# All eight feature pairs of one group's first layer as seven half-size products, with a new written order of the whole kernel

## The chip, the cores and the metric

The kernel runs on one core of one Trainium2 chip. The metric is the device time of one execution in microseconds (us). Timed runs of the kernel before give a median of 292.01 us (291.48 to 292.09, three runs). The profile comes from one more execution, which took 292.66 us; the span of its instructions, from the first to the last, is 290.9 us.

## What is computed

Attention with two kinds of window (q, k, v: 8 batches, 8 heads, 576 positions, 64 features a head), then two matrix layers with a Silu between them. Cut to what matters:

```python
scores = scale * np.matmul(q, k.transpose(0, 1, 3, 2))
# heads 0-3: rel in [0, 32); heads 4-7: rel in [0, 128) and rel % 4 == 0
scores = np.where(masks[None], scores, -1e9)
attn = softmax(scores); attn_out = attn @ v
x = attn_out.transpose(0, 2, 1, 3).reshape(4608, 512)
h = x @ w_in                      # 512 x 2048
g = h * (1.0 / (1.0 + np.exp(-h)))
return g @ w_out                  # 2048 x 512
```

All operands of the matrix engine are float16 on the chip, sums are float32.

## The kernel before, in words

**Stages.** The 8 batches of attention feed a table of features xA (128 partitions, 4 parts of the 512 features, a ring of 2048 tokens). The 4608 tokens are worked off in ten groups: groups 0 and 1 of 256 tokens, groups 2 to 9 of 512. For each group, layer 1 makes gT (16 blocks of 128 hidden features by the group's tokens) and layer 2 makes the output rows. Attention of later batches runs between the matrix layers of earlier groups. Batches 0 to 2 bring their operands into shape by transposes on PE, batches 3 to 7 by a cast into DRAM (POOL's queue) and transposing DMAs (SP's queue). Batches 5 to 7 also send their result to DRAM and take it back transposed (steps W and X, SP's queue).

**Two ways of layer 1.** A standard block (`l1`, line 834; matmuls on line 839) is four matmuls of the group's width (512 columns for group 7), one for each part of the 512 features, and then one Silu on ACT (line 848) or, in mode t, a Tanh on ACT and a DVE instruction (lines 851 and 853). A fast pair (`l1_fast`, line 894; matmuls on line 927) makes two blocks at once by the seven products of Strassen's scheme: the blocks' weights, the features and the tokens are each cut in half, and seven products of two matmuls of 256 columns take the place of eight such half products (eight matmuls of 512 columns). The scheme needs sums of weight halves S1 to S4 (steps a0, a2, a4, a6, each for two pairs, line 879) and of feature halves T1 to T4 (steps t7, t8, t9, line 890). Products 0, 2, 4 and 6 of a pair go to its first bank of PSUM, products 1, 3 and 5 to its second. Products 0 to 2 are copied out (line 935, by ACT or DVE as the order says), and after products 3, 4 and 5 a DVE addition (line 943) joins one of the copies to what the bank holds by then. ACT applies Silu to three pieces: 256 columns after product 6 (line 939), 256 after product 4 (946) and 512 after product 5 (949). So a product must wait until the reader of the product two before it has left the bank. Which pairs are fast is set by `FAST1`: pairs 4 to 7 of group 7 and all eight of groups 8 and 9.

**Layer 2.** From group 2 on it uses the same scheme (`layer2_fast`, line 1013; line 1024), with sums of gT as steps u (line 990, mostly DVE). Results are added on DVE (line 1050) into output buffers ob, three in rotation, and stored from SP's or ACT's queue (line 1059; line 1052 for halves of the last tile).

**The order.** Nothing is scheduled by a program: `TABLE` is a list of steps, and each engine and each queue gets its instructions in that order. A step's name is given several times: the first time issues its matmuls, the next times its followers on the other engines, one each. What stands after "=" is, the first time, the PSUM bank (a, b, x, y, u, z; s is a double bank; a fast pair names two banks and a digit for its set of temporaries), and later the engine or queue (A: ACT, D: DVE, P: POOL, S: SP). `l7.4.0=by1` is product 0 of pair 4 of group 7; `l7.2=a` and `l7.2=s` are a standard block and its Silu; `7S1` are scores of batch 7, with exp on ACT and a mask multiplication on DVE; `7P0` and `7D0` are products with v; `7XP0`, `7XD0`, `7W0`, `7X0` bring features out; `7T` is one transposing DMA and `7L` loads for batch 7; `y7.0.3` is product 3 of tile 0 of group 7's layer 2; `f6` is a one-element copy on POOL that reads gT (a fence); `z` with a number is a filler: one idle matmul of 512 columns (line 1091) that keeps PE's clock up while it waits.

Of the kernel before, what the change touches and what calls it, by code (L numbers as in the profile page):

```python
# [11 lines left out]
0N0=D z15 z2 0N1=A z1 z25 0N3=D z21 z0 0TD2=b 0N2=A 0TD1=z 0TD1=A 0TD2=D 0TD3=x 0TD3=A 0TD0=u 0TA1k=a 0TD0=D  # L12
0TA1k=A 0S3=s 0S3 0TA1q=x 0TA0q=z 0TA0q=D z9 0TA1q=A 0TA0k=a 0TA0k=A 0S3 0S4=s 0S4 0S0=bz 0S4 0D0=u 0S1=s 0S0
0S0 0D1=z 0TR=x 0D0 0D1 0O0 0D0 0S1 0TR=A 0S1 0P1=b 0TR=A 0S6=au 0S6 0S5=s 0N10=D 0S6 0S5 0S5 0N6=D 0P0=a
0TS0=x 0D1 0TS0=A 0P1 0P1 0TS1=b 0O2 0D2=u 0P0 0D4=z 0TS1=A 0TS1=A 0P0 0TS0=A 0XP1=b 0XP1=A 0S2=s 0D2 0D2 0S2
0D4 0XP2=a 0D4 0O1 0XP0=u 0S2 0XP0=A 0D3=b z28 0XD0=y 0XD0=A 0D3 0D3 0P3=x 0P3 0P2=u 0P2 0XP2=A 0XD0=A l0.0=b
0P2 0P3 0XD1=u 0XD1=D 0XD1=D l0.0=s 0M 0XP3=a l0.3=z l0.7=x 0XP4=b 0XP4=D 0XP5=u 0XP5=D l0.7=t 0B 0XP3=D
l0.3=s l0.1=y l0.7 l0.6=b l0.1=s l1.6=z l1.6=t l1.4=a l1.4=t 0N7=D l0.2=u l1.6 l0.6=t l0.6 l1.11=y l1.11=s
l1.4 l1.7=z l0.2=s l1.3=x l1.7=s l1.0=y l0.8=b l0.11=u l1.0=s 0N4=A l0.8=s l0.11=t l0.11 l0.9=y l1.10=z l0.9=s
l1.3=s l1.10=s l1.8=b l1.1=u l0.5=x l1.15=a l1.1=s l1.15=s l1.2=y l0.5=s l1.9=u l1.9=s 0N8=D l1.12=x l0.13=a  # L20
l1.12=s 1TD3=z l1.8=s l1.2=s l0.12=x l0.12=t l0.4=b l0.4=s 1TD3=D l0.13=t l0.12 0B 1TD1=u 1TD1=D 1TS1=y 1TS1=A
0N5=A 1TA1q=z l0.13 1TS1=A l1.5=b 1TD2=u 1TA1q=A l1.5=s 1TD0=x l0.14=y 1TD2=D l0.14=s l0.10=a l0.10=s 1TD0=D
1TA1k=x 1TA0q=b 1S3=s 1S3 1TA1k=D 1TA0q=D 1TA0k=u 1TA0k=D 1TS0=x y0.1.0=z 1TS0=D 1TS0=D 1S1=au 1S1 1V1=D 1O2
1S2=bx 1S2 1S3 y0.0.0=y 1S3 1S2 1S2 1S4=s l0.15=a 1S1 1S4 l1.14=b l1.13=u 1V0=D 1S4 1S4 1S0=s l0.15=t y0.0.1
y0.1.1 l0.15 1D1=a 1S1 l1.14=s 1D1 1D1 1D2=x y1.0.0=b y1.0.1 1D4=a 1D4 l1.13=s 1D0=u y0.1.2 1S0 1S0 1S0 1D4
1D2 y0.1.3 1D0 1D0 1D2 y0.0.2 y0.0.3 1O0 y0.0.3=A 1P3=u 1P3 w1 1P0=x 1P0 0N9=D y1.0.2 1P0 y1.1.0=y 0B 1P3
1P1=x y0.1.3=A 1XP0=a 1P1 1P1 1XP0=D 1P2=z 1P2 y1.0.3 1P2 y0.0.3=A 1D3=u y1.1.1 y1.0.3=A 1D3 1XP2=z 3T 1XP1=a
3T 1D3 1XP2=D 1XD0=b 1XP1=A 1XD0=D 1XD0=A 1XD1=u y1.1.2 1XD1=D 1XD1=D 1XP3=x 1XP3=A 1XP5=z 1XP5=D 2TD0=b
2TD1=a 2TD2=z 2TD3=u 2TD2=D 2TD1=A 2TD3=A y1.1.3 2TD0=D 1XP4=a 2S4=s 1XP4=D y1.1.3=A 2TA0k=b 2TA0k=D 2S4
2TA1k=a 3T 2TA0q=z 2TA1q=y 2S4 2TA1q=D 2TA0q=A 2TS1=x 2TS0=u 2TS0=A 2TS1=D l2.10=b 2S3=s 2TS1=A 2TS0=A 2V1=D  # L30
2S2=zy l2.10=t 2S3 2S3 2S2 2TA1k=D l2.0=x 2S2 l2.10 2S1=ba 2S3 2S1 2S1 2S0=s 2S0 2S4 l2.8=u 2S2 l2.8=s l2.2=y
l2.2=s 2V0=D 2D1=z l2.1=b 2D1 2D1 l2.14=a l2.1=s l2.6=z l2.6=s l2.3=u 2S0 2S1 l2.3=s 2D0=b l2.14=t 2S0 w0
2D2=y l2.4=z l2.4=s 3T w1 w1 2D0 2D0 l2.0=s w0 l2.15=u l2.15=s l2.5=z l2.5=s 2D2 2D2 l2.14 2P1=b y1.0.3=A 2P1
2P0=y 2P1 l2.11=u l2.11=s 2XD0=x 2P2=b w0 l2.7=z l2.7=s 2P0 2P0 l2.12=y 2P2 2P2 y0.1.3=A 2XP1=b 2D4=u 2XD0=A
2XD0=A l2.9=a u2.2=D l2.12=s 2D4 y1.1.3=A 2D4 l2.9=s 2XP1=D l2.13=z l2.13=s 3L 2D3=x 2XP2=b 2XP2=A 2XP0=u
u2.0=D y2.0.0=y 2D3 2D3 y2.0.0=D 2XP0=A 2XP3=x 2XP3=D 2XD1=a 2P3=z 2P3 2XD1=A u2.2=D 3S1=s u2.0=D 2XD1=A v0
# [36 lines left out]
6P3 y6.0.2=A u6.1=D y6.0.3 y6.0.4 7S2 7S2 y6.0.4 7S4=s 7S4 7D0=b y6.0.3 a4=D 7P0=y 7D0 y6.0.6 6P3 y6.0.6=A 7D0
# [44 lines left out]
def kernel(  # L118
# [1013 lines left out]
```

## Time and profile before

| | |
|---|---|
| median of three runs | 292.01 us (291.48 to 292.09) |
| the profiled execution | 292.66 us |
| its span | 290.9 us |
| TensorE clock granted, mean | 0.998 |
| matmuls | 3034, the last one starts at 287.2 us |
| line 839 (standard blocks) | 480 matmuls, 352 of 512 columns |
| line 927 (fast pairs) | 280 matmuls of 256 columns |
| DVE, ACT busy | 217.9, 189.3 us |

PE is the matrix engine and PEld its weight loads, DVE the vector engine, ACT the one for functions, POOL the general one, SP the one that only issues DMAs. In the timeline and in the chain, the columns are the start, the duration and what ran. The chain follows the work that ended last back to what released each step. A matmul's own duration includes its way through the array (379 ns for 512 columns, 273 for 256), so its rate is read from starts.

### The profile page before, as it was taken

How to read it: one execution, taken by the hardware profiler on the slowest of the kernel's cores; microseconds unless marked ns; L12 is line 12 of the kernel's file. 1: busy time of each engine (PE TensorE's matmuls, PEld its weight loads, DVE VectorE, ACT ScalarE, POOL GpSimd, SP SyncE). 2: the span in 40 equal slices, each digit the busy share in tenths (PEclk: the TensorE clock that was granted, in tenths of full speed). 3: DMA queues.
4: the chain of work that ended last, by engine and by line, in shares of the span. 5: the costliest groups of instructions: out<-in, count | busy, mean ns of one | idle time of the engine just before them, and what ended most of it. 6: DMA issues, size and time to landing. Idle time of an engine off the chain costs nothing.

```text
span 290.9 us, 7524 instructions
## 1 busy us (share of the span) xinstructions
PE 284.4 (98%) x3034; PEld 205.5 (71%) x3034; DVE 217.9 (75%) x584; ACT 189.3 (65%) x400; POOL 57.3 (20%) x93
## 2 busy tenths in 40 slices
PE   8999999999999999999999999999999999999994
PEld 3578855745665787467477756678578888888884
DVE  5493477789886995744986686598889997759962
ACT  6887892697688459657962684475757654518920
POOL 7854634000910150023000270000100000000000
PEclk9999999999999999999999999999999999999999
DMA  8999999999999999970999899946252511111003
GB/s 162 184 204 196 190 193 190 203 190 182 172 171 188 241 115 211 206 146 7 198 163 173 214 136 190 273 105 161 77 115 61 85 75 72 73 74 73 2 32 114
DMA packets 98731, 42.31 MB, mean 145 GB/s; under 512 B 67208, under 2 KB 94344, under 8 KB 98696
## 3 DMA queue, kind: packets, MB, share of 16 engines
q0 software_dynamic: 46464, 19.21, 54.2%
q1 hardware_dynamic: 49640, 18.03, 30.3%
q10 hardware_dynamic: 2592, 4.59, 4.6%
q8 instruction: 24, 0.39, 0.5%
q14 instruction: 11, 0.09, 0.1%
HBM read 39.19 MB, written 17.10 MB: 194 GB/s over the span
## 4 chain that ended last, share of the span: by engine, by line
PE 59%; DMA 2%; DVE 2%; ACT 0%; issue 0%; DVEq 0%; ACTq 0%
PE y L1024 27%; PE h L839 17%; PE h L927 11%; DMA out_dram<-ob 2%; PE av_D L710 1%; PE s L636 1%; PE av_P L710 1%; DVE ob L1050 1%; DVE oD L718 0%; PE xd L752 0%; DVE nat L506 0%; PE xp L736 0%; DVE work L990 0%; DVE gT L990 0%; DVE rcps L716 0%
## 5 line engine op out<-in xcount | busy, mean ns | idle before, releaser
L839 PE MATMUL h<-xA,w_in 128*128 128x512 f16 (+1 forms) x480 | 99.0, 351 | 0.3 <-ACT xA L504 0.3
L839 PEld LDWEIGHTS <-w_in 128*128 128x128 f16 x480 | 44.1, 98 | 32.6 <-DVE oP L718 0.3
L848 ACT ACTIVATE gT<-h 128x512 f16<-128x512 f32 (+1 forms) x98 | 50.7, 547 | 23.3 <-PE h L839 22.7
L1024 PEld LDWEIGHTS <-gT 128*128 128x128 f16 x512 | 48.8, 98 | 7.1 <-issue 0.6
L1024 PE MATMUL y<-w_out,gT 128*128 128x256 f16 x384 | 48.4, 273 | 0.0
L1024 PEld LDWEIGHTS <-work 128*128 128x128 f16 x384 | 36.6, 98 | 5.8 <-DVE work L990 0.3
L1024 PE MATMUL y<-w_sum,work 128*128 128x256 f16 x256 | 31.9, 273 | 0.1
L1050 DVE TENSOR_TENSOR ob<-y,nat 128x256 f32<-128x256 f32 x48 | 19.9, 420 | 14.2 <-PE y L1024 8.3
L710 PEld LDWEIGHTS <-probs 128*128 128x128 f16 x448 | 21.5, 97 | 8.7 <-issue 0.5
L718 DVE TENSOR_TENSOR oD<-av_D,rcps 72x384 f16<-72x384 f32 (+1 forms) x40 | 22.8, 575 | 1.3 <-PE xd L752 0.5
L504 ACT COPY nat<-y 128x256 f32<-128x256 f32 x31 | 11.5, 372 | 18.5 <-PE y L1024 10.9
L644 ACT ACTIVATE probs<-s 128x960 f16<-128x960 f32 (+4 forms) x24 | 21.1, 881 | 3.3 <-PE s L636 3.0
L653 DVE TENSOR_TENSOR probs<-probs,mask 128x960 f16<-128x960 f16 (+2 forms) x35 | 21.2, 628 | 2.5 <-ACT probs L644 1.4
L649 ACT ACTIVATE probs<-s 128x480 f16<-128x480 f32 (+4 forms) x36 | 18.1, 564 | 2.5 <-PE s L636 2.5
L853 DVE SCALAR_TENSOR_TENSOR gT<-th,h 128x512 f16<-128x512 f32 (+1 forms) x22 | 12.7, 583 | 8.4 <-ACT th L851 8.4
L718 DVE TENSOR_TENSOR oP<-av_P,rcps 96x384 f16<-96x384 f32 x32 | 17.3, 547 | 1.2 <-PE xp L736 0.6
L1024 PE MATMUL y<-w_sum,gT 128*128 128x256 f16 x128 | 16.6, 273 | 0.4 <-DVE ob L1050 0.4
L716 DVE RECIPROCAL rcps<-av_D 72x6 f32<-72x6 f32 (+1 forms) x40 | 7.5, 189 | 12.5 <-PE av_D L710 12.5
L1024 PE MATMUL y<-w_out,work 128*128 128x256 f16 x128 | 16.6, 273 | 0.0
L504 ACT COPY ob<-y 128x256 f32<-128x256 f32 (+1 forms) x15 | 6.4, 432 | 15.7 <-PE y L1024 7.0
L1085 POOL COPY fence<-gT 128x1 f16<-128x1 f16 x11 | 3.2, 306 | 64.6 <-ACT gT L848 25.7
L504 ACT COPY vraw<-h 128x256 f32<-128x256 f32 x32 | 11.2, 374 | 6.8 <-PE h L927 5.5
(133 smaller groups left out, 484.6 us busy)
## 6 DMA issues: line engine op xcount, KB each, us to landing
out_dram<-ob ACTq DMA_DIRECT2D x17, 256.0 KB, 2.6
out_dram<-ob SPq DMA_DIRECT2D x17, 256.0 KB, 2.5
kq_s<-in_k_dram POOLq DMA_DIRECT2D x5, 576.0 KB, 9.8
kq_s<-in_q_dram POOLq DMA_DIRECT2D x5, 576.0 KB, 12.2
vp<-in_v_dram POOLq DMA_DIRECT2D x6, 384.0 KB, 7.3
w_out<-in_moe_w_out_dram POOLq DMA_DIRECT2D x4, 512.0 KB, 10.4
vraw<-in_v_dram POOLq DMA_DIRECT2D x10, 160.0 KB, 5.8
w_in<-in_moe_w_in_dram POOLq DMA_DIRECT2D x3, 512.0 KB, 9.8
```

The source lines that it names most:

```text
L504: nc.scalar.copy(dst, src)
L644: nc.scalar.activation(p2, both[:, :, :n], AF.Exp, scale=scale)
L649: nc.scalar.activation(p2[:, i], sp[i][:, :n], AF.Exp, scale=scale)
L653: nc.vector.tensor_tensor(p2, p2, mk[:, None, :].broadcast_to([P, 2, n]), ALU.mult)
L710: nc.tensor.matmul(a[:, f - f0, : rhs.shape[1]], lhs, rhs, start=True, stop=True)
L718: nc.vector.tensor_tensor(o[:, f0:f1], a[:m, :, :D], rcp.broadcast_to([m, N, D]), ALU.mult)
L839: nc.tensor.matmul(h[:, :w], w_in16[:, c, f * P : (f + 1) * P], x_g[:, c], start=(c == 0), stop=(c == HP - 1),)
L848: nc.scalar.activation(o, h[:, :w], AF.Silu, scale=2.0)
L853: nc.vector.scalar_tensor_tensor(o, th[:, :w], 1.0, h[:, :w], ALU.add, ALU.mult)
L927: nc.tensor.matmul(y, lhs[:, c, j], rhs[:, c], start=first and c == 0, stop=c == 1, skip_group_check=not first,)
L1024: nc.tensor.matmul(y, lhs[:, c, tb * P : (tb + 1) * P], rhs[:, c], start=first and c == 0, stop=c == KP - 1, skip_group_check=not first,)
L1050: nc.vector.tensor_tensor(half, y, (u2, t5, t1)[n - 3], ALU.add)
```

## The change

`FAST1` gives group 7 all eight pairs, and `TABLE` is written anew from the first step to the last. Nothing else differs. Group 7's standard blocks `l7.0` to `l7.7` are gone, and pairs `l7.0.0` to `l7.3.6` are new. The lines of the order that matter most (its start, with the fillers; the stretch of group 7's layer 1; its end):

```diff
-0N0=D z15 z2 0N1=A z1 z25 0N3=D z21 z0 0TD2=b 0N2=A 0TD1=z 0TD1=A 0TD2=D 0TD3=x 0TD3=A 0TD0=u 0TA1k=a 0TD0=D
...
-y6.0.5 a6=D y6.0.5 6X0 l7.2=a l7.6=z l7.1=x silu l7.6=s 7P0 6W3 l7.2=s l7.1=s 7S4 7S3 7P0 l7.4.0=by1 t7 t7
-7P1=u 7P1 7P1 7S4 l7.4.1 l7.4.1=A 6W1 7D2=z l7.3=a l7.3=s a6=D 7D2 l7.4.0=A l7.5.0=s2 7D2 7W0 f6 l7.0=x
-y6.0.5=S 7D1=a a0=D l7.0=s l7.4.2 t7 7D1 7D1 6X1 l7.4=u 7P3=z 7P3 l7.5.0=A 7P3 l7.4=s l7.4.3 l7.4.2=A l7.5.2
...
-y9.1.3 y9.1.2=D y9.1.4 y9.1.3 y9.1.5 y9.1.4 y9.1.6 y9.1.5 y9.1.5=S y9.1.6=A y9.1.6=A
+z24 0N1=D z11 z7 z23 0N0=A 0N2=A z1 0N3=D 0TD2=x 0TD3=u 0TA0k=a 0TD3=D 0TA1k=b 0TD0=z 0TD2=D 0TD1=u 0TD0=A
...
+l7.1.0=uy1 l7.1.0=A 6W3 y5.1.6=S y6.0.5 6X1 t7 7D0 t7 y6.0.5=A t7 y6.0.6 t7 y6.0.6=A l7.0.0=ab0 l7.0.1 l7.1.1
+l7.2.0=s2 7D2=x l7.1.2 l7.0.0=A l7.1.1=A 7D0 l7.0.2 l7.1.3 7D2 l7.0.1=A l7.0.3 l7.1.2=A l7.1.4 l7.2.0=A l7.2.1
+7D2 l7.4.0=zx1 l7.0.2=A l7.1.3 l7.0.3 l7.1.5 l7.0.4 l7.2.2 f5 l7.1.4 l7.0.5 silu l7.1.4 l7.1.6 l7.1.6 l7.4.1
...
+l7.0.4 f6 l7.4.5 a2=P l7.4.4 l7.4.6 7D3 l7.3.2=A l7.3.3 l7.3.4 l7.2.3 l7.4.4 l7.4.5 l7.2.4 l7.3.5 l7.3.5
...
+y9.0.6 y9.0.5 y9.1.0=D y9.1.2 y9.0.5=S y9.1.1=D y9.1.3 y9.1.2=D y9.1.4 y9.1.3 y9.0.6=A y9.1.5 y9.1.4 y9.0.6=S
+y9.1.6 y9.1.5 y9.1.5=S y9.1.6=A y9.1.6=A
...
-    FAST1 = {7: 4, 8: 8, 9: 8}
+    FAST1 = {7: 8, 8: 8, 9: 8}
```

More of the change, by code (lines that the diff above doesn't have):

```diff
@@ L17 @@
[L17 to L36, printed above, removed]
@@ new lines @@
+u2.2=D u2.2=D 3S1=s 3S1 l3.5=a y2.0.1=D 3S1 u2.1=D l3.0 y2.0.2 3S2=xb 3S2 u2.0=D u2.1=D y2.0.2=D 3S0=s v1 3S0
+y2.0.3 3S0 y2.0.3 l3.1 y2.0.4 3S2 l3.5=t l3.15=x 3S0 3S4=s l3.5 3S3=bz l3.15=t 4T 4T 4T y2.0.4 3V1=D 3S2
+y2.0.5 y2.0.5 y2.0.6 3S3 3S3 2XP4=z 2XP4=D l3.15 3S4 y2.0.6=A l3.14=b 3S1 l3.2=y l3.14=s l3.9=z l3.9=s l3.3=b
+3P2=x l3.3=s u3.2=D 3P2 3P2 l3.7=u 3P3=b l3.6=z y2.0.5=A l3.7=s 3P0=a 3P3 l3.6=s 3P3 l3.2=s 3S3 3P1=b l3.8=u
+l3.8=s 4T l3.12=x 3V0=D u3.2=D l3.12=t y2.1.0=u 3P1 3P0 3D0=z y2.1.0=A 3S4 3S4 3P1 y2.1.1=b 3XP2=y u3.0=D
@@ new lines @@
+l3.12 4V0=D 3D0 4V1=A l3.11=x l3.11=s 3D0 3XP2=D 3P0 3D1=z 3D2=y l3.13=a l3.13=s 3D1 y2.1.2 y2.1.2=A 3D1
+y2.1.1=D 3XP5=z y2.1.3 u3.2=D y2.1.4 3D2 3D2 u3.1=P 3XP3=x 5L y3.0.0=y 5L 3XP3=A y2.1.3 y2.1.5 4S0=s 3XP3=A
+4S0 4S0 3XP5=D u3.1=D u3.1=D y2.1.4 3D4=z 3XP1=x u3.0=D y2.1.5 y2.1.6 3D3=a y2.0.6=A 3D4 3XP1=A 3XP0=b
+y2.1.5=S 3D4 y3.0.1=z y2.1.6=A 4S2=s y3.0.1=A u3.0=D y3.0.0=D 4S4=ux 4S2 4S4 5L 3D3 u3.0=D y3.0.2 4S2 u3.1=D
+u3.2=D y3.0.3 3XP0=D y3.0.2=A 4S4 3D3 y3.0.4 4S1=ab 4S1 4S1 4S3=s 3XD0=x 3XD0=A 3XD1=u y3.0.4 3XD1=A 3XD0=A
@@ new lines @@
+4XP5=D y3.1.0=A u4.0=D 4P2=z y3.1.1=D 4XD0=y 4P2 5V1=A 4XD0=A y3.1.2 4XD0=A y3.1.2=D y3.1.3 y3.1.4 4XP1=x
+4XP1=D 6L 5S1=s 5S1 4P2 5S3=yb 6L y3.1.4 5S1 5S3 5S3 l5.10=x y3.1.3 y3.1.6 5S2=s y3.1.5 l5.10=t y3.1.6=D
+u4.1=P u4.1=D 5S2 5S2 l5.10 l5.9=a l5.9=t 5S2 5S4=s 5S0=bx 6V0=D 6L l5.9 5S0 4D4=z 5S0 5S0 y3.1.5 5S4 l5.11=y
+l5.11=s 5S3 l5.15=b l5.15=s u4.2=D y3.1.5=S l5.14=a l5.14=s 4D4 4D4 u4.2=D l5.13=u l5.5=x l5.13=s 5S4 5S4
+l5.3=b u5.2=D u4.0=D y3.0.6=S y3.1.6=A u4.1=D 4D3=z f1 4XP4=u 4XP4=A u4.1=D l5.5=s l5.4=a l5.4=s l5.3=s l5.7=u
@@ new lines @@
+u5.2=D l5.8=a 5D0=x 5S1 y4.0.0=y 4D3 5P3=b 5D0 l5.7=s 4D3 5P1=z 5D0 y4.0.1=u 5D2=x u4.0=D l5.8=t 5P3 5P3
+y4.0.0=A y4.0.2 5P1 l5.12=b l5.8 4XD1=a l5.12=s 5P1 y4.0.1=D 4XD1=A y4.0.2=D y4.0.3 y4.0.4 4XD1=A 5D2 5D2
+y4.0.3 5D1=z 4XP3=a 4XP3=A y4.0.4 5D1 5P0=x 5P0 y4.0.5 5P2=a 5P0 6T 5P2 l5.6=b 5D1 6T 5W0 y4.0.5 5P2 y4.0.5=A
+y4.0.6 y4.0.6=A 5W2 u5.2=D l5.6=s l5.1=u u5.1=P l5.1=t l5.1 l5.2=a l5.2=s 5D3=z l5.0=x l5.0=t y4.1.0=b
+y4.1.1=a y4.1.0=A y4.1.1=A u5.1=D u5.1=D 5D3 5D4=y 5D3 y4.1.2 5D4 5D4 l5.0 y4.0.6=A y4.1.2=D 5W1 6S0=s 6S1=uz
@@ new lines @@
+6V1=D 6T y4.1.3 y4.1.4 y4.1.3 6S1 y4.1.5 u5.0=D u5.0=P 6S0 6T 6S0 6S1 6S3=yx 6S4=s 5X0 5W3 6S3 y4.1.4 7L
+6S2=zu y4.1.5 y4.1.6 6S2 6S3 y4.1.6=A l6.2=y 6S4 6S2 l6.1=z l6.2=s l6.7=a l6.7=s l6.12=u l6.4=x l6.1=s l6.3=b
+l6.3=s l6.12=s 6S2 6S0 6S3 y4.1.5=S y4.1.6=S a4=D l6.15=y 6D2=b 7L 6S4 6S4 l6.15=t y5.0.0=a 6S1 l6.11=u 7L
+l6.15 y5.0.0=A 6P0=y l6.4=s a0=D 7V1=A u5.0=D u5.0=D 6P0 6P0 l6.0=z l6.11=s l6.0=t 7V0=A l6.14=x l6.14=s 7T
+l6.0 l6.10=u 6D2 6D2 6D1=y y5.0.1=z y5.0.1=A 6D0=x 6D1 u5.1=D l6.5=b u6.2=P u6.2=D l6.5=t u5.2=D y5.0.2
@@ new lines @@
+l7.6.0=ab0 7D4 t8 7P2=z y6.1.1=D t8 l7.3.4 f7 l7.5.1 7P2 l7.4.5 l7.6.0=A l7.7.3 l7.6.1 7P2 l7.5.1=A y6.1.3
+l7.6.1=A y6.1.2=A l7.5.0=D l7.2.4 l7.5.3 l7.6.2 y6.1.3 l7.7.5 l7.6.3 l7.6.2=A l7.6.3 l7.5.2 l7.5.2=A l7.7.5
+l7.6.4 l7.6.4 l7.2.5 y6.1.5 l7.5.3 y6.1.5 l7.6.5 l8.0.0=zy0 l7.6.5 l7.5.4 u7.0=P l7.5.5 l8.0.1 l7.7.4 l7.5.4
+l7.6.6 l7.7.5 y6.1.4 l8.0.0=A l8.0.2 l8.0.1=A l7.6.6 l8.1.0=ax1 l8.0.3 l7.5.6 l7.6.5 l8.1.0=A l7.6.4 t8 y6.1.4
+l7.5.6 l8.1.1 l7.5.5 l8.1.1=A l8.1.2 l8.1.2=A u7.0=D y6.1.6 u7.0=D l8.0.2=A l8.1.3 l8.2.0=s2 l8.2.1 t8
@@ new lines @@
+l8.2.0=A l8.0.3 l8.0.4 l8.2.1=A l8.1.3 l8.0.4 l8.1.4 l8.1.5 y6.1.6=A y6.1.6=S l7.5.4 l8.1.4 l8.2.2 l8.0.4
+l8.0.5 l8.2.2=D f8 l8.0.6 l8.1.6 l8.2.3 l8.2.4 l7.5.5 u7.2=P l8.0.6 l8.1.6 u7.0=D l8.4.0=bz1 y7.0.0=u l8.1.5
+l8.4.0=A y6.0.6=S l8.2.4 u7.1=P l8.4.1 l8.0.5 l8.1.4 u7.1=D l8.3.0=ax0 l8.3.1 l8.2.3 l8.2.6 l8.2.4 l8.4.1=A
+l8.2.6 l8.3.1=A y7.0.1=y u7.1=D u7.2=D l8.4.2 l8.3.3 l8.3.0=A y7.0.0=A y6.1.5=A l8.2.5 l8.2.5 u7.2=D l8.4.2=A
+l8.3.2 l8.1.5 l8.5.0=s2 7W3 u7.1=D l8.5.0=D y7.0.2 7W1 7X1 l8.3.2=A l8.4.4 y7.0.1=D l8.4.4 l8.3.4 u7.2=D
@@ new lines @@
+l8.4.3 l8.5.1 l8.0.5 l8.3.4 l8.3.3 y7.0.2=A l8.3.4 y7.0.3 l8.3.6 y7.0.4 l8.2.5 y7.0.3 y7.0.4 l8.4.3 l8.3.5
+y7.0.5 y7.0.5 l8.3.6 l8.5.2 y7.0.6 l8.4.5 y7.0.5=S y7.0.6=A y7.1.0=a l8.3.5 l8.3.5 l8.5.1=D l8.7.0=uy1 l8.5.3
+l8.5.2=A l8.4.5 l8.7.0=A u8.0=P y7.1.0=D l8.7.1 l8.5.4 l8.4.6 l8.4.6 l8.7.1=D l8.6.0=zb0 l8.5.3 l8.7.2
+l8.7.2=A l8.6.0=A l8.5.4 l8.7.3 l8.6.1 l8.4.5 l8.6.1=A y7.1.1=x l8.7.3 l8.4.4 y7.1.1=D y7.0.6=S l8.5.6 l8.5.6
+l8.5.5 l8.7.4 t9 l8.7.4 l8.5.5 y7.1.2 l8.7.4 l8.6.3 l8.5.5 u8.1=P u8.1=D y7.1.3 u8.1=D l8.7.5 l8.6.2 l8.7.5
@@ new lines @@
+l9.4.5 l9.4.4 l9.6.0=yb0 l9.5.1 l9.4.5 l9.6.0=D l9.2.5 l9.6.1 l9.5.0=A l9.4.4 l9.3.4 l9.3.5 u9.0=P l9.5.1=A
+u9.0=P l9.5.2 l9.5.2=A l9.7.0=zu1 l9.6.2 l9.5.3 l9.6.2=D l9.7.0=A l9.6.1=A l9.5.3 l9.7.1 l9.5.4 l9.7.1=A
+l9.5.4 l9.4.5 l9.6.3 l9.6.3 l9.7.2 l9.5.5 l9.5.4 l9.7.2=A l9.6.4 l9.7.3 l9.4.4 l9.5.5 l9.5.5 l9.6.4 l9.6.4
+l9.3.6 l9.7.3 l9.6.5 l9.4.6 l9.6.5 l9.7.4 l9.7.5 l9.7.4 l9.7.5 u9.0=D l9.5.6 l9.6.6 l9.7.6 l9.6.5 u9.1=P
+l9.7.5 l9.7.4 y9.0.0=b l9.6.6 u9.2=P l9.7.6 y8.0.6=S y9.0.1=u u9.1=D u9.2=D y9.0.0=A y9.0.1=A u9.1=D u9.2=D
```

127 lines of the change are left out of this document (52 added, 75 removed).

## The prediction

> **What bounds the kernel now.** I read the busy line first, then the waits, then the chain in order of time, then busy time by stage.
>
> ```profile
> PE 284.4 (98%) x3034; PEld 205.5 (71%) x3034; DVE 217.9 (75%) x584; ACT 189.3 (65%) x400; POOL 57.3 (20%) x93
> ```
>
> PE is busy for 98% of 290.9 us. "Busy" alone could be padding, so I look at starts, in the timeline of PE and in the chain:
>
> ```profile
> 232.09 0.38 PE L927 MATMUL h<-xA,kqT 128*128 128x256 f16 x2
> 232.31 0.38 PE L927 MATMUL h<-xA,w_in 128*128 128x256 f16 x2
> 232.53 0.38 PE L927 MATMUL h<-nat,nat 128*128 128x256 f16 x2
> 232.75 0.38 PE L927 MATMUL h<-nat,kqT 128*128 128x256 f16 x2
> ```
> ```profile
> 115.07 4.32 PE h L839 x20
> ...
> 263.95 8.35 PE h L927 x74
> 272.30 0.03 issue
> 272.33 2.01 PE h L927 x16
> ```
>
> A half-size product (two matmuls of 256 columns) starts every 0.22 us, 109 ns a matmul. Twenty matmuls of 512 columns take 4.32 us, 216 ns each. Laying 109, 216 and the like for the small shapes (39 for 96 columns, 29 for 72 and 65) along the written order gives 278.1 us of matrix work; the last matmul starts at 287.2. So PE waits or runs cold for some 9 us, 8 of them before 24 us. After that it loses only about 1 us more, most of it at the end: 74 matmuls at 109 would take 8.07 and take 8.35, 16 take 2.01 for 1.74. Anything that shortens PE's stream therefore shortens the span, and any wait put into it lengthens the span.
>
> One wait in the middle is worth a line (waits, then chain):
>
> ```profile
> DVE ob L1050 <- DMA out_dram<-ob: 1.5, 1, 1.5
> ```
> ```profile
> 105.86 7.25 DMA out_dram<-ob
> ...
> 113.21 0.44 DVE ob L1050
> 113.64 0.04 issue
> 113.68 1.03 PE y L1024 x8
> ```
>
> An addition into an output buffer waits for the store that last used it (three buffers in rotation), and PE starts its next product 0.58 us late at 113.68.
>
> **The change, part by part.** The sum is against the profiled execution (292.66 us, span 290.9); the three runs shown have a median of 292.01, and I carry the difference over to it.
>
> *Products.* Four pairs of group 7 lose two blocks of four 512-column matmuls each (8 x 216 = 1.73 us) and gain seven products of two 256-column ones (14 x 109 = 1.53 us): 0.20 a pair, **-0.81**. Weight loads go from 8 to 14 of 98 ns, 1.37 us, under 1.53. Where products already run this way the loads fill 20.62 of 23 us and PE keeps up:
>
> ```profile
> 195.00:222.00 27.00, 27.00 (x294) 20.88 (x292) 23.94 (x64) 17.05 (x38) 1.39 (x3) 1.00 0.43 102
> 222.00:245.00 23.00, 23.00 (x213) 20.62 (x212) 20.32 (x57) 15.53 (x46) 0.66 (x3) 1.00 0.33 84
> 245.00:272.00 27.00, 27.00 (x247) 23.89 (x245) 21.89 (x64) 14.36 (x41) 0.00 (x0) 1.00 0.16 60
> ```
>
> (Columns: stretch, its length, then busy us and instructions of PE, loads, DVE, ACT, POOL, the clock, DMA.) [...]
>
> *Evictions.* Each pair drops two Silu over 512 columns (599 ns each) and adds three copies (374 on ACT, 422 on DVE), three DVE additions (420) and Silu of 385, 415 and 632. The order gives 19 of group 7's 24 copies to ACT. In a queue, instructions start some 86 ns (DVE) to 115 (ACT) before the one ahead ends, so an addition costs the queue 0.33. Counted along the order from group 7's first product to group 8's, DVE has 15.5 us beside 17.3 of matrix work (before 15.0 beside 17.6), ACT 12.8 (10.0). Neither exceeds PE. What gets tight is the handover inside a pair: product i+2 writes the bank that product i's reader must have left. Of group 7's 40 such handovers 11 leave under 0.5 us beyond the reader's own duration, the least 0.28. Group 9 before has 12 of 40 under 0.5, least 0.24, and the rows at 263.95 lose 0.28 us to them. I take **+0.3**; bounds 0 and 3.2, with two additions (0.67) queued ahead at each of the eleven (room 0.38 on the mean: 11 x 0.29).
>
> *Weight and feature sums.* All four weight-sum steps and group 7's sums exist before as well; they move. Group 7's first product needs no sum and only old features, and the turn of the next features (6X0), which stood right ahead of the first block, now has 7 us of matrix work before the sums: nothing. One weight sum (a2, the fourth) goes to POOL: 2.12 us for twice its size, so 1.06 by halving, and it stands 0.2 us of matrix work before product l7.3.4 that reads it. POOL has nothing else to do then, so it can start when its fence is met, some 3 us earlier: nothing, at worst 1.9.
>
> *Fillers.* Eight idle matmuls become five. Five of the old six in front wait for a load at 6.06 anyway. The other two ran at 9.03 and 17.92 between real work, 0.31 and 0.43 us. Input weights land in a fixed series (20.4, 23.0, 25.6 us) and the order now wants the last two slices 0.6 and 2.4 us of matrix work earlier, which leaves the start about no slack; but the shift of v that held an early product at 12.74 for 0.6 us is now ahead. **-0.4**; bounds -0.65 and +0.5.
>
> *Output buffers.* In the old order eight reuses come within 4.4 us of matrix work after the store's issue, the one at 113 after 2.9. In the new order three do; the same place has 5.4. **-0.5**; bounds -0.58 and 0.
>
> *Masks.* Products with v now stand close behind the DVE mask that they read: 0.47 to 0.67 us too close before 1P1, 2D1 and 2P1, where the old order has one case of 0.36 (7D0) that cost nothing, since DVE ran ahead of the order by 0.14 on the median. **+0.3**; bounds 0 and 1.8.
>
> *The tail.* The store of the last group's first tile (256 KB) moves from ACT's queue (283.05) to SP's, behind the two half stores of 285.05 and 285.93 and ahead of a last one. Such a store lands 2.5 us after issue and the DMA share is 0.36 there: **+0.2**; bounds 0 and 0.75.
>
> ACT's table loads stay 16 (exp and Silu alternate equally often). Sum: -0.81 + 0.3 - 0.4 - 0.5 + 0.3 + 0.2 = -0.9. The rest of the rewritten order I could weigh only by such distances; elsewhere its bank handovers are as wide as before (least 0.24 to 0.27 us of room in both, after the start), so nothing, but I round the gain down: -0.8, **291.2 us**.
>
> **Rivals.**
> - *The waits eat it (292.0).* If masks and handovers cost 0.7 more than taken, PE's shorter stream stands still where it was shortened. For: DVE 90% of PE's work in group 7's stretch against 81% in group 9's (21.89 of 27), where PE did lose time; against: 85% there before with none lost.
> - *DVE late in group 7 (293.2).* If a sum or a product with v holds DVE's queue while the pairs run, each tight handover stops PE. It decides from two additions queued ahead: all eleven cost 3.2, half 1.6, giving 292.8 to 294.4. For: from 180 to 190 us of matrix work the new order puts 10.8 us on DVE against 10.3 on PE, so DVE may come late into the pairs; against: before holds 10.6 on 10.0 at 60 and PE lost nothing.
> - *Half-size products don't pay (292.4).* From 123 ns a matmul (1728/14) the gain is gone. At 130, as the eight of 113.68 took with their pipeline's end (1.03 us), the pairs lose 4 x (14 x 130 - 1728) = 0.37 instead of gaining 0.81: 292.4. Against: nine tenths of the 1303 matmuls of 256 columns start the next within 110. [...]
>
> That the change does nothing is excluded: the order names all seven products of all eight pairs.
>
> **Chances.** A measurement of this kernel tells 0.2% (0.58 us) from no change. Forecast, the new order no worse than the old: 0.50, by itself 290.1 to 291.4. Waits eat it: 0.28, within 291.4 to 292.6. DVE late: 0.20; half-size products: 0.02. So faster 0.50, same 0.28, slower 0.22. The range goes down to all favourable bounds (-0.81 - 0.65 - 0.58 = -2.0, 290.0) less a little, and up to 293.2, where half of the slow case is in.
>
> **What would show it.** Right: h under L927 with 336 matmuls (280 before) and under L839 with 32 fewer than 480; start to start still 109; no wait of DVE for a store of ob near 105 to 113; PE's last matmul starting about 286.2. Handovers: L943 and L949 with idle time of PE behind them between 204 and 221. Masks: gaps of PE before av at some 47, 62 and 68 us. Tail: more than 3.7 us from the last matmul's start to the end. Wrong: PE idle of 0.5 us or more between 195 and 225, or more than the old 8.0 us lost by 24 us.

## The result and the profile after

Twenty executions of the kernel after have a median of 289.61 us (288.83 to 292.92), twenty of the kernel before 291.82 us (291.15 to 293.35). The ratio is 0.9943 (95% interval 0.9918 to 0.9968), so about 1.7 us off; the forecast had 0.8. (Times 292.01, from which the forecast started, the ratio gives 290.3.) The medians differ by 2.2 us. Both can hold, since the ratio goes by the means (290.18 and 291.84 us) and the times after lie in two heaps: thirteen from 288.83 to 290.01 us, seven from 291.26 to 292.92.

The profiled execution took 292.35 us, so it comes from the upper heap, and its span is 290.6 us against 290.9 before. The page's busy line, then the groups of matmuls (their columns: count, busy us, mean ns of one, idle time before them):

```profile
PE 281.0 (97%) x3055; PEld 207.1 (71%) x3055; DVE 221.3 (76%) x594; ACT 196.9 (68%) x422; POOL 60.3 (21%) x95
...
L843 PE MATMUL h<-xA,w_in 128*128 128x512 f16 (+1 forms) x448 | 90.6, 349 | 0.0
...
L931 PE MATMUL h<-xA,w_in 128*128 128x256 f16 x96 | 17.3, 272 | 0.0
L931 PE MATMUL h<-nat,nat 128*128 128x256 f16 x96 | 16.7, 272 | 0.0
```

Lines stand four further down than before (839 is 843, 927 is 931, 1050 is 1054), because the order is four lines longer. The standard blocks have 448 matmuls where they had 480; the two largest groups of the fast pairs have 96 each where they had 80, and all of line 931 has 336 where 927 had 280. PE is busy 3.4 us less and yet the span is only 0.3 us shorter. Where PE stands is in the chain of work that ended last (start, duration, what ran):

```profile
105.13 0.44 DVE ob L1054
105.58 7.97 DMA out_dram<-ob
114.01 0.43 DVE ob L1054
114.48 1.91 PE y L1028 x16
...
265.10 6.99 PE h L931 x62
272.09 3.09 PE h L931 x26
275.18 12.27 PE y L1028 x112
287.47 0.37 ACT ob L508
```

The store that DVE waited for before is still in the chain, at the same place, and takes 7.97 us where it took 7.25. The timeline of that moment shows both stores leaving and both additions coming late:

```profile
105.51 0.36 ACTq L1063 DMA_DIRECT2D out_dram<-ob  x1
105.58 0.33 SPq L1063 DMA_DIRECT2D out_dram<-ob  x1
...
113.67 0.76 DVE L1054 TENSOR_TENSOR ob<-y,nat 128x256 f32<-128x256 f32 x2 [4.15 <-DMA out_dram<-ob]
...
114.48 0.71 PE L1028 MATMUL y<-w_out,gT 128*128 128x256 f16 x5 [2.26 <-DVE ob L1054]
```

DVE stands for 4.15 us (1.5 before) and PE starts its next product 2.4 us late (0.58 before). So the wait that the forecast took away has grown. At the end it is the other way round. The 88 matmuls of pairs from 265.10 to 275.18 (62 and 26) take 10.08 us for 9.59 at 109 ns, about as in the old order, but then 112 of layer 2 run in one piece, 12.27 us for 12.21. In the chain of before the same layer is broken by additions and copies, and PE starts at 282.66 0.26 us late:

```profile
280.85 0.44 DVE ob L1050
...
282.23 0.38 ACT nat L504
...
282.66 4.54 PE y L1024 x40
```

**A table of lost time.** To compare stretches I take, for each matmul, its start less the matrix work that stands ahead of it in the order (216 ns for 512 columns, 109 for 256, 39, 29 and the like for the small ones, as in the prediction; idle matmuls count as lost). How much this grows in a stretch is what PE lost there. The first column is the loss up to 28 us, the last what lies between the start of the last matmul and the end of the span. (The 287.2 us that the table of before and the prediction give for the start of the last matmul is its end; it starts at 286.9.)

```
                    work    to 28  28-62  62-104 104-118 118-195 195-222 222-end  tail   span
before            276.35     9.75  -0.73    0.30    0.51   -0.37    0.11    1.10  3.98  290.9
before, half st.  276.35     9.25  -0.73    0.31   -0.07   -0.35    0.09    1.09  3.41  289.2
after             275.54     8.90  -0.11    0.10    2.34   -0.18   -0.01    0.69  3.42  290.6
after, again      275.54     9.70  -0.47    0.18   -0.08   -0.27    0.10    0.69  3.42  288.7
after, third      275.54     8.83   0.47    0.14   -0.08   -0.28    0.10    0.68  3.42  288.7
after, early st.  275.54     8.93  -1.02    0.09   -0.08   -0.27    0.10    0.68  3.37  287.2
 the same, again  275.54     8.66  -0.53    0.09   -0.08   -0.27    0.09    0.68  3.38  287.5
stores left out   275.54     9.03  -0.85    0.11   -0.08   -0.27    0.10    0.68  3.55  287.7
pairs as blocks   276.35     8.99  -0.75    0.10   -0.08   -0.27    1.45    0.69  4.63  291.0
product 0 twice   276.41     8.59  -1.02    0.02   -0.02   -0.27    0.09    0.69  3.36  287.7
new start         276.35     9.02  -0.81    0.32   -0.07   -0.35    0.10    1.10  5.03  290.6
no two fillers    276.35     9.06  -0.72    0.32   -0.08   -0.35    0.10    1.10  3.37  289.0
new end           276.35     9.38  -0.72    0.30   -0.06   -0.35    0.10    2.51  4.74  292.1
new rest          275.54     9.95  -0.73    0.30   -0.06   -0.36    4.92    0.72  3.37  293.5
```

(Small negative numbers come from matmuls of few columns that start a little faster than the values used: between 28 and 62 us of before, the 96 matmuls of 96 columns whose weights are 96 by 64 start 27 ns apart on the mean.) A matmul at a border can fall to either side, which moves 0.1 us from one column to the next. All rows but before and after are the experiments that follow. Where a kernel's steps are the same, 222-end stands still to a hundredth and 195-222 within some 0.1; three columns move from execution to execution of one kernel: the start, 28-62 and 104-118. In these three PE waits for DMAs: in the second profile of after it starts 1.16 us late at 8.08 us, for a load of k, and the other two columns are shown below.

### The profile page after: what moved, and what is told of

Read it like the earlier page. It is cut to its first block, busy times and chain, and to the rows that moved or that the text cites. A ratio compares the mean times of both kernels' runs of the same rounds, so it can differ in the third digit from the quotient of the medians.

```text
span 290.6 us, 7628 instructions
## 1 busy us (share of the span) xinstructions
PE 281.0 (97%) x3055; PEld 207.1 (71%) x3055; DVE 221.3 (76%) x594; ACT 196.9 (68%) x422; POOL 60.3 (21%) x95
## 4 chain that ended last, share of the span: by engine, by line
PE 85%; DMA 10%; DVE 2%; POOL 2%; issue 0%; ACT 0%; DVEq 0%
PE y L1028 33%; PE h L843 27%; PE h L931 13%; PE y L967 4%; DMA w_out<-in_moe_w_out_dram 4%; DMA out_dram<-ob 3%; PE s L640 2%; PE av_D L714 2%; DMA nat<-in_q_dram 2%; PE av_P L714 2%; DMA w_in<-in_moe_w_in_dram 2%; PE xp L740 1%; POOL vp L332 1%; PE xd L756 1%; PE td L557 0%
## 5 line engine op out<-in xcount | busy, mean ns | idle before, releaser
L843 PE MATMUL h<-xA,w_in 128*128 128x512 f16 (+1 forms) x448 | 90.6, 349 | 0.0
L843 PEld LDWEIGHTS <-w_in 128*128 128x128 f16 x448 | 41.2, 98 | 29.9
L852 ACT ACTIVATE gT<-h 128x512 f16<-128x512 f32 (+1 forms) x83 | 43.1, 547 | 20.7 <-PE h L843 20.0
L857 DVE SCALAR_TENSOR_TENSOR gT<-th,h 128x512 f16<-128x512 f32 (+1 forms) x29 | 16.8, 583 | 11.8 <-ACT th L855 11.4
L648 ACT ACTIVATE probs<-s 128x960 f16<-128x960 f32 (+4 forms) x25 | 22.2, 888 | 3.6 <-PE s L640 3.5
L508 ACT COPY ob<-y 128x256 f32<-128x256 f32 (+1 forms) x19 | 8.0, 422 | 19.9 <-PE y L1028 14.5
L508 ACT COPY vraw<-h 128x256 f32<-128x256 f32 x44 | 15.6, 378 | 6.9 <-PE h L931 5.5
L855 ACT ACTIVATE th<-h 128x512 f32<-128x512 f32 (+1 forms) x29 | 15.0, 522 | 6.6 <-PE h L843 5.8
L931 PE MATMUL h<-xA,w_in 128*128 128x256 f16 x96 | 17.3, 272 | 0.0
L931 PE MATMUL h<-nat,nat 128*128 128x256 f16 x96 | 16.7, 272 | 0.0
```

Of the source, the lines that this page charges most:

```text
L508: nc.scalar.copy(dst, src)
L648: nc.scalar.activation(p2, both[:, :, :n], AF.Exp, scale=scale)
L843: nc.tensor.matmul(h[:, :w], w_in16[:, c, f * P : (f + 1) * P], x_g[:, c], start=(c == 0), stop=(c == HP - 1),)
L852: nc.scalar.activation(o, h[:, :w], AF.Silu, scale=2.0)
L857: nc.vector.scalar_tensor_tensor(o, th[:, :w], 1.0, h[:, :w], ALU.add, ALU.mult)
L931: nc.tensor.matmul(y, lhs[:, c, j], rhs[:, c], start=first and c == 0, stop=c == 1, skip_group_check=not first,)
```

## The experiments

**Theory:** PE's stream is the bound, the four pairs bring their 0.81 us whole, the new start and the new end bring some tenths each, and the kernel after pays, in some executions only, for two stores that land late. **Rivals:** the heaps come from something else, such as input loads at the start; the gain is all in the order and none in the products.

### Does the wait for output buffers make the upper heap?

Two versions of after. In the first (early stores) one store's token moves, so that it leaves some 13 us earlier, and another store is cut in two:

```diff
-3D3=a y2.0.6=A 3D4
+3D3=a 3D4
...
-y2.0.5=A l3.7=s
+y2.0.5=A y2.0.6=A l3.7=s
...
-                if last and n < 5:
+                if (last and n < 5) or (g, tb, n) == (2, 1, 3):
                     nc.sync.dma_start(out=out[row : row + P, DH:], in_=half)
-                rows, src = (out[row : row + P, :DH], half) if last else (out[row : row + P], ob)
+                rows, src = (out[row : row + P, :DH], half) if last or (g, tb, n) == (2, 1, 5) else (out[row : row + P], ob)
```

> The kernel after, with the two stores that the additions at 113.7 us wait for issued earlier: the store of y2.0.6 stands right behind its sister's on ACT's queue (some 15 us earlier), and the right half of tile 1 of group 2 is stored by itself from SP right after its addition (some 2.6 us earlier); the left half follows at the old place. Theory (the wait for output buffers is what splits the times of the kernel after into a group at 288.8 to 290.0 and one at 291.3 to 292.9): the additions wait no longer, the upper group is gone, median 288.9 us (288.7 to 289.3). Rival (the two groups come from something else, such as when the input weights land at the start): the two groups stay, median 289.6 and highest above 291.3.

Measured: 289.33 us (288.85 to 289.97, six executions), ratio to before 0.9916 (0.9899 to 0.9932). The second leaves the two stores out:

```diff
-                (nc.sync if eng == "S" else nc.scalar).dma_start(out=rows, in_=src)
+                if (g, tb, n) not in ((2, 0, 6), (2, 1, 5)):
+                    (nc.sync if eng == "S" else nc.scalar).dma_start(out=rows, in_=src)
```

> The kernel after without the two stores (tile 0's second half-pair of rows and tile 1's first, of group 2; 256 of 4608 output rows are left unwritten), everything else as it stands. Theory (output buffers split the times): as with the earlier stores, one group only, 288.8 us (288.5 to 289.2), and DVE's wait for a store near 110 us is gone. Rival (the split comes from elsewhere): two groups as after, median 289.6. If this one has no upper group and the earlier stores still have one, the traffic of the stores at that moment counts, not only the buffers.

Measured: 289.78 us (288.97 to 290.88, six), 0.9933 (0.9910 to 0.9956). No time of either lies above 291.2, and PE loses nothing between 104 and 118. The timeline of the early stores: the two additions now wait for PE's product alone.

```profile
104.69 0.33 SPq L1056 DMA_DIRECT2D out_dram<-ob  x1
...
110.25 0.76 DVE L1047 TENSOR_TENSOR ob<-y,nat 128x256 f32<-128x256 f32 x2 [1.62 <-PE y L1021]
```

The two medians are higher than the 288.9 and 288.8 that I expected and lie outside the ranges given, and 290.7 and 290.9 occur without the stores: some 1.5 us vary for another reason, so the rival has a part.

For the lower heap of after itself I took a second profile:

> The kernel after once more, unchanged, for a second profile. Theory: where its time lies in the lower group (288.8 to 290.0), DVE's wait for a store near 110 us leaves PE no gap or a short one, under 0.5 us; where it lies in the upper group, PE stands for 2 us or more at 112. Rival: the gap at 112 is there in the lower group as well.

It took 290.46 us, which lies between the heaps. In its timeline the same two stores leave together, but land within 5.2 us (at 111.06 and 111.28), before the additions ask:

```profile
106.02 0.36 ACTq L1056 DMA_DIRECT2D out_dram<-ob  x1
106.08 0.33 SPq L1056 DMA_DIRECT2D out_dram<-ob  x1
...
111.65 0.76 DVE L1047 TENSOR_TENSOR ob<-y,nat 128x256 f32<-128x256 f32 x2 [1.62 <-PE y L1021]
```

PE loses nothing there; what this execution is slower by, it lost at the start (9.70 us to 28). So the additions ask 5.6 us after the stores leave, and these two stores take 3.7 to 8.3 us from one execution of after to the next. Loads of batch 5 into vp and kq_s are under way all that time (issued at 103.5 to 105.7 in the first profile, landed by 111.6 to 118.6). In four profiles the time of SP's store goes with its place beside the load of k into kq_s: where it left behind that load, by 0.64 us in the first profile of after and 1.09 in before, it took 7.97 and 7.25 us; where it left ahead of it, by 0.62 and 0.32 us in the second and third of after, 5.20 and 4.37. That the loads slow the store is likely, but no run changed them alone.

Then both once more, beside each other on one chip:

> The kernel after with the earlier stores, once more, beside the kernel after on one chip. Theory: no time above 290.2 us, median 289.2.

> The kernel after, unchanged, beside the run with the earlier stores. Theory: its lowest times are those of the run with the earlier stores (288.8 to 289.0), and some three in ten lie above 291.2, where PE stands at 112 us; the median lies 0.2 to 0.8 us above that of the run with the earlier stores. Rival: no such upper group on this chip, medians equal.

Measured: early stores 289.07 us (288.89 to 289.23, five), 0.9910 (0.9893 to 0.9926); after 289.75 us (289.13 to 293.28, twelve), 0.9946 (0.9917 to 0.9975), with two at 293.27 and 293.28, fewer than the three in ten that I expected. Over all executions, nine of 33 of after lie above 291.2 us and none of eleven with the early stores, nor of the six without the stores. The theory holds for the heap as a whole. That all nine stood at 112 us isn't shown: one of the nine has a profile. The three highest (292.92, 293.27 and 293.28) have a mean granted clock of 0.993 to 0.994, the other six 0.999 to 1.000. The last section has a run in which 3.4 us at half clock took about that much off the mean (0.994 in its profiled execution), so a longer stand may have cost these three the clock as well; no profile shows it.

The third profile of after, at 290.5 us and again between the heaps, names the other thing that varies. PE waits at 52 us for the load of batch 2's q:

```profile
52.13 0.21 PE L550 MATMUL td<-ident_w,nat 96*128 96x96 f16 x1
...
53.72 0.37 PE L550 MATMUL td<-ident_w,nat 96*128 96x96 f16 x5 [1.38 <-DMA nat<-in_q_dram]
```

Five profiles with the new order lose 0.28, 0.64, 1.54, 0 and 0.50 us at this place (the two with early stores come last). The last of the loads lands at 50.9 to 53.6 us in both orders; the old one asks for it at 54.0 to 54.5, the new one at 52.0 to 53.0. In the 28-62 column the old order's loss is -0.73 in both rows, the new one's -1.02 to 0.47.

**The same store in the old order.** Only the cut of the store in two, on the kernel before:

> The kernel before, with the right half of tile 1 of group 2 stored by itself right after its addition. Theory: the wait of 0.58 us at 113 is gone, so 291.8 - 0.5 = 291.3 us (291.0 to 291.6) with a narrower spread. Rival (that wait costs nothing on the whole since a later one takes its place): 291.8.

Measured: 291.32 us, 0.9988 (0.9977 to 0.9999): 0.35 us gained, and the 0.51 of the 104-118 column is gone. So before paid for this store too. The spread isn't clearly narrower: eleven of twelve executions lie from 291.01 to 292.23 us, one at 296.20 us with a mean clock of 0.983, which is not in the ratio. The half store has a side effect: it waits for its data in SP's queue ahead of a transposing DMA, which leaves at 102.69 us (97.73 in before), and POOL's loads of batch 5 follow some 6 us later than in before. So this run takes the loads away from the store as well as giving the buffer more room.

### What the four pairs bring

**Pairs back to blocks**, in the order of the early stores: `l7.0.0=ab0` becomes `l7.0=a`, `l7.0.3` becomes `l7.1=b`, each with one Silu, the other tokens of the pair go, and so on for pairs 1 to 3. (Blocks `l7.4` and `l7.5` take the halves of the double bank, for which the kernel gets a small helper.)

```diff
-l7.0.0=ab0
+l7.0=a
...
-l7.0.0=A
+l7.0=s
...
-l7.0.3
+l7.1=b
...
-l7.0.5
+l7.1=s
...
-    FAST1 = {7: 8, 8: 8, 9: 8}
+    FAST1 = {7: 4, 8: 8, 9: 8}
```

> The kernel after with the earlier stores, and pairs 0 to 3 of group 7 as eight standard blocks again, each at the place of its pair's product 0 or 3 in the new order. It weighs the seven products alone. Theory (a half-size product costs 218 ns of PE's stream and the handovers inside the pairs cost nothing, since PE lost 0.0 us against its matrix work between 195 and 222 us): 0.81 us slower than with the earlier stores, 289.7 us if those give 288.9. Rival 1 (the handovers take back 0.3 of it, as predicted): 0.5 slower. Rival 2 (all of the gain is the order's, not the products'): no slower, within 0.2 us.

Measured: 291.89 us (291.05 to 293.36), 1.0006 (0.9988 to 1.0024): not 0.8 but 2.6 us slower than the early stores. Its row of the table says why: work 276.35 (the 0.81), but the stretch 195 to 222 loses 1.45 where it lost 0.10, and its profiled tail is 4.63. The timeline of PE shows two of four waits of the stretch, both on ACT, whose Silu over 512 columns now stand ahead of what others need:

```profile
214.25 0.37 PE L703 MATMUL av_D<-vd,probs 128*128 128x65 f16 x7 [0.30 <-ACT gT L944]
...
216.28 0.38 PE L932 MATMUL h<-nat,kqT 128*128 128x256 f16 x2 [0.30 <-ACT vraw L497]
```

The experiment mixes the products' price with that of my placing of the blocks, and doesn't tell between theory and rival 1. It speaks against rival 2 only by the work column: 0.81 of the 2.6 us is work, and 1.35 is the new waits.

**A cleaner price:** product 0 of the four pairs twice over, everything else as with the early stores.

```diff
-            for c in range(2):
+            for c in (0, 1) * (2 if (g, i) == (7, 0) and j < 4 else 1):
```

> The kernel after with the earlier stores, and product 0 of pairs 0 to 3 of group 7 computed twice over (two more matmuls of 256 columns each; the second overwrites the first), so that these four pairs cost PE 4 x 2 x 109 = 0.87 us more, about what the old blocks cost over the seven products (0.81). Nothing else changes. Theory (PE's stream is the bound there, each matmul counts whole): 0.87 us slower than with the earlier stores, 290.2 us if those stay at 289.3. Rival (PE has slack against ACT or DVE there, so that the saving of the four pairs was not in the time): under 0.3 slower.

Measured: 289.80 us (289.52 to 290.10), 0.9938 (0.9924 to 0.9951). Against the two runs of the early stores (0.9916 and 0.9910, each beside before on its own chip) that is 0.0025 of 291.6, 0.7 us, for 0.87 us of added matmuls. The times alone leave it wide, since the intervals of the ratios just overlap. The table settles it for PE: work is 0.87 up, and the stretch 195 to 222 loses 0.09 as it does without them, so nothing there takes the added matmuls up. The windows view of the stretch (stretch, length, then busy us and count of PE, loads, DVE, ACT, POOL, clock, DMA), early stores first, product 0 twice second:

```profile
195.00:222.00 27.00, 27.00 (x305) 24.02 (x303) 25.30 (x72) 20.02 (x54) 1.61 (x4) 1.00 0.37 92
```
```profile
195.00:222.00 27.00, 27.00 (x305) 24.13 (x304) 24.44 (x70) 19.40 (x53) 1.61 (x4) 1.00 0.35 87
```

DVE is busy for up to 94% of 27 us and still doesn't set the pace: what PE is given more, its stream takes longer. PE is the bound there, and what the pairs save in matmuls is in the time.

### What the new start brings

The kernel before with the half store, once with the first 182 steps in the new order, once without the two fillers that stood among real work:

```diff
-0N0=D z15 z2 0N1=A z1 z25 0N3=D z21 z0 0TD2=b 0N2=A
+z24 0N1=D z11 z7 z23 0N0=A 0N2=A z1 0N3=D 0TD2=x 0TD3=u
...
```

> The kernel before (four fast pairs, its stores as in the run with the half store) with the first 182 steps of the new order, fillers included, in the place of the steps that they do; the rest in the old order. It weighs the new start alone: 17 us of matrix work, to some 27 us. Theory (the new start is worth what the two profiles show by 28 us: 9.25 us lost in the run with the half store, 8.93 in the new order): 0.3 us faster than that run, 291.0 us (290.8 to 291.2). Rival 1 (the start was worth more, as in the first pair of profiles, 9.75 against 8.90): 290.5. Rival 2 (the loads' landing sets it anyway): 291.3, no change.

Measured: 290.81 us (290.23 to 292.34), 0.9971 (0.9959 to 0.9983), 0.5 us faster than with the old start (0.9988): between the theory's 0.3 and rival 1's 0.8. The two intervals overlap, so the gain is likely, and its size is not fixed by the times.

```diff
-0TA0q=D z9 0TA1q=A
+0TA0q=D 0TA1q=A
...
-0D3=b z28 0XD0=y
+0D3=b 0XD0=y
```

> The kernel before with the half store, without its two fillers among the real work (at 9.03 and 17.92 us). It weighs the term of -0.4 that the prediction gave to the fillers. Prediction's reading (the two stand on PE's path with 0.31 and 0.43 us): 0.4 us faster than with them, 290.9 us. Rival (what follows them waits for DVE or for a load that lands at its own time): no change, 291.3.

Measured: 291.14 us, 0.9985 (0.9975 to 0.9995): 0.1 us less than with them. With these intervals that is told neither from none nor from the predicted 0.4. The profile lost 9.06 us up to 28, where four with the old start lose 9.25 to 9.95. The timeline of PE says more, with the fillers first, without them second:

```profile
17.42 0.38 PE L1084 MATMUL y_warm<-w_sum 128*128 128x512 f16 x1
...
18.11 0.53 PE L703 MATMUL av_P<-vp,probs 128*128 128x65 f16 x12
```
```profile
18.02 0.52 PE L703 MATMUL av_P<-vp,probs 128*128 128x65 f16 x12 [0.27 <-DVE vp L681]
```

Without the filler PE waits for DVE's `vp` and starts the same product 0.09 us earlier. It is alike at the first filler: the scores that follow it start at 9.20 us for 9.31. So in this profile the fillers stood where PE waits anyway, as the rival has it, and most of the start's gain would be the order of its steps.

### What the new end brings, and two seams

Two kernels with the old order up to a place and the new one behind it: from group 9's fourth pair on (new end), and from 196 us on (new rest, with all eight pairs).

```diff
-l9.3.0=ub0 l9.2.6 l9.2.6 l9.2.5 l9.1.3 l9.3.0=A l9.4.0=xz1
+l9.3.0=au0 l9.3.1 l9.3.0=A y8.1.5=S l9.4.0=xz1 l9.4.0=D
...
```

> The kernel before with the half store, up to where group 9's fourth pair begins (some 266 us); from there the steps stand in the new order. Four fast pairs in group 7, as before. It weighs the new order's end alone, for which the prediction gave nothing. Theory (in every profile so far the old order loses 1.1 us after 222 us and the new one 0.7): 0.4 us faster than the run with the half store alone, 290.9 us (290.7 to 291.1). Rival (the end's gain hangs on what the new order does earlier in groups 8 and 9, or is lost in the last store): 291.3, no change.

> The kernel before with the half store, up to some 196 us; from there the steps stand in the new order, with all eight pairs of group 7 fast. Its difference to the run with the new end alone is what the four pairs bring, without the new start. Theory (products count whole, handovers cost next to nothing): 0.8 faster than that run and 1.2 faster than the half store alone, 290.1 us (289.9 to 290.4), with some tenths for the seam. Rival 1 (the handovers take 0.3 back, as the prediction has it): 290.4. Rival 2 (the pairs bring nothing): 290.9, as with the new end alone.

Measured: 293.07 us, 1.0052 (1.0032 to 1.0073), and 295.21 us, 1.0111 (1.0084 to 1.0137). Both expectations failed, and for one reason: at the seam, products stand whose readers the two orders had put elsewhere. In the first, two products of group 9 wait for DVE and start 1.2 and 0.5 us late (most of the rest of this profile's loss is its tail of 4.74 us):

```profile
265.39 0.38 PE L920 MATMUL h<-xA,w_in 128*128 128x256 f16 x2 [1.05 <-DVE vd L936]
...
266.36 0.38 PE L920 MATMUL h<-xA,w_in 128*128 128x256 f16 x2 [0.37 <-DVE vd L936]
```

In the second, PE waits twice for DVE (`oD` at 198.58 us, `ob` at 199.94) and loses 4.9 us from 195 to 222, 4.7 of them by 205; behind that it loses 0.72 to its last matmul, as after does, where before loses 1.10. So the end's 0.4 us is a steady reading of thirteen profiles (1.09 to 1.10 in four with the old end, 0.68 to 0.72 in nine with the new one; the run with the seam at 266 left out) and is not shown by a time. In before, 0.26 of it is the late start at 282.66 and 0.13 another at 274.96; the new end has neither.

## Why the prediction was right, and where it was not

Direction and mechanism were right: PE's stream is the bound and got shorter. The gain was about twice the 0.8 us forecast. The three costs that the sum held (+0.3, +0.3 and +0.2) came to nothing, and an end that it gave nothing gained 0.4. Of the signs named beforehand, the 336 matmuls, 448 under the standard blocks and starts 109 ns apart came; no wait for a store near 105 to 113 us came in two of three profiles of after, in which the last matmul starts at 285.3 us, and not in the first, where it starts at 287.2; none of the signs of the rivals came. By the prediction's terms, beside what was measured:

- **Products, -0.81: right.** Matrix work along the order went from 276.35 to 275.54 us, matmuls of 256 columns still start 109 ns apart, and added matmuls there lengthen PE's stream one to one (the time by 0.7 us for 0.87). The rival "half-size products don't pay", for which a matmul had to take 123 ns or more, is out.
- **Handovers, +0.3: nothing.** From 195 to 222 us the new order loses -0.01 to 0.10 us, the old one 0.09 to 0.11. Room of 0.28 to 0.5 us behind a reader was enough each time. The rival "DVE late in group 7" didn't occur, though DVE is busy for 25.3 of 27 us there.
- **Sums moved, 0: right.** No wait on a weight or feature sum stands in that stretch, that on POOL included.
- **Fillers, -0.4: right in sign, probably for the wrong part.** The start is worth 0.5 us by the experiment and 0.6 by the profiles (four old starts lose 9.25 to 9.95 by 28 us, 9.58 on the mean; nine new ones 8.59 to 9.70, mean 8.96). The two fillers alone bring 0.1 by the times, with an interval that still holds 0.4; by the one profile without them, PE waits in their place.
- **Output buffers, -0.5: this step failed in the upper heap** (nine of 33 executions, one of them with a profile). It said "eight reuses come within 4.4 us ... In the new order three do; the same place has 5.4", with 2.9 in the old. The distance was taken from the place in the order where the store stands. But here the store leaves when its data are ready: in before the addition ends at 105.84 and SP's store starts at 105.86, some 2.9 us ahead of its place in the order. Taken from the traces, DVE asks 5.8 us after the store's issue before (105.86 to 111.68), and 5.6 after. So the room hardly changed. And by the prediction's own rows the wait was not gone: the store shown there takes 7.25 us, more than the 5.4 that it gave the new place. What did change is the cost of a late store. Before, one addition waits, DVE stands for 1.5 us and PE loses 0.58 of it; after, two additions wait for two stores that leave together, and nearly all their delay reaches PE (the additions start 2.5 us later than 5.6 us after the stores, PE 2.4 late). A store of 7.25 us cost PE 0.58 before, one of 7.97 costs 2.4 after; one of 5.2 costs nothing. The bound of no gain, in "bounds -0.58 and 0", left out that the wait could get longer. Where the stores land in time, the wait is gone, as forecast.
- **Masks, +0.3: nothing.** Between 40 and 100 us no product with v starts over 0.01 us late in any of seven profiles of the new order.
- **Tail, +0.2: nothing.** The chain ends with ACT's last copy and store, issued behind all of SP's; the tail is 3.4 us with the new place of that store and, in an undisturbed end, with the old one.
- **"Elsewhere nothing": two things.** The new end loses 0.4 us less. And the new order asks for batch 2's q some 2 us earlier and waits up to 1.5 us for it: the rival "waits eat it" in another place than named.

Added up for a typical execution of the lower heap: -0.81 (pairs), -0.6 (start), -0.4 (end), -0.35 (the store, as in the half-store run), -0.15 (62 to 104, by the table), and +0.2 for the load of batch 2 (column 28-62: -0.73 to a mean of -0.53 over eight profiles) make -2.1, beside the medians' -2.2. The upper heap takes part of that back in the ratio.

The version with the early stores is faster than both kernels: 289.10 us over its eleven executions, against 289.62 for 33 of after.

## What to carry to other kernels

Measure a buffer's room from when the data of its store are ready to when the next writer asks, in the trace, not from places in a written order (here SP's store left 2.9 us ahead of its place), and set it beside the longest time that such a store takes. Where a DMA's time varies from one execution to the next (here 3.7 to 8.3 us for two stores), a wait with little room can split the times in heaps, and one profile shows one heap; read the spread before the profile. When two orders are to be weighed against each other, add or double one cost inside one of them; putting halves of the two together can add a seam that costs more than what is sought, as both seams did here.

## What the runs showed of the hardware

**The clock fell after a short stand.** At the seam of the run with the new rest PE worked little from 196.9 to 199.9 us (waits of 1.65 and 1.16 us), and then at half speed to 203.1; the clock fell at 199.7, so it was halved for 3.4 us. The windows view, with the granted clock in the third column from the right:

```profile
198.00:200.00 2.00, 0.26 (x5) 0.15 (x7) 2.00 (x6) 0.00 (x0) 0.00 (x0) 0.92 0.00 0
200.00:201.00 1.00, 1.00 (x16) 0.77 (x16) 1.00 (x3) 0.48 (x1) 0.00 (x0) 0.50 0.22 86
201.00:202.00 1.00, 1.00 (x7) 0.61 (x5) 0.03 (x1) 0.60 (x2) 0.00 (x0) 0.50 0.96 276
202.00:203.00 1.00, 1.00 (x16) 0.57 (x15) 0.08 (x1) 0.49 (x2) 0.00 (x0) 0.50 0.88 177
203.00:204.00 1.00, 1.00 (x10) 0.90 (x9) 1.00 (x3) 0.92 (x2) 0.00 (x0) 0.96 1.12 192
```

Eight matmuls of 256 columns started 213 ns apart there, not 109. The single stand of 2.4 us in the kernel after left the clock at 1.00. At the seam it fell 2.7 us after the end of the last full run of matmuls, with one matmul of 72 columns in between. From what length of a stand on it falls, and what ends the half clock, no run shows. The waits at this seam cost more than their length: of the 4.9 us lost some 3.2 are the stands and 1.6 the half clock. Five of this run's six executions have a mean clock of 0.988 to 0.994 and take 294.67 to 295.99 us; the sixth has 1.000 and takes 293.57.

**The first matmuls were slow.** In before the idle matmuls of 512 columns from 1.59 to 6.29 us start 427 ns apart, in after those from 1.60 to 4.16 us; the next start 216 or 217 ns apart, from 6.69 and 4.47 us on. (The clock column of the windows view reads 1.00 in both stretches.) Behind the last matmul the column gives a mean of 0.84 for 288.00 to 290.90 us of before, where PE has nothing to do. The fillers are meant to keep the clock up; for the two among the real work no run shows that they do: the run without them has mean clocks of 0.998 to 1.000, as has the run with them but for the one execution at 0.983.

**The end varies by itself.** The tail is 3.36 to 3.55 us in ten of fourteen profiles and 3.98 to 5.03 in four, whatever the order. In before's 3.98 a half store took 3.8 us to land, in after's 3.42 the same one took 1.7.
